# The row-maximum selector product of a fused attention and soft mixture-of-experts kernel, moved from fp32 to fp32r

## The chip, the cores and the metric

The kernel runs on one core of one Trainium2 chip. The metric is the device time of one execution in microseconds; the time before is 1116.34 us, the median of three runs (1116.29, 1116.34 and 1117.21).

## The reference, cut to what matters

There are B = 4 images with C = 128 channels. Keys and values are one and the same array: kv is averaged over 4 x 4 pixels, which leaves 768 keys for each image, and multiplied by a 128 x 128 matrix. Each of the 12288 queries of an image attends to its image's 768 keys. The result x (49152 rows of 128) goes through a soft mixture of experts with 8 experts of 4 slots.

```python
k = v = pool4x4(kv) @ w_sr
s = (q @ k.T) / sqrt(C)
s = s - s.max(-1)                      # the row maxima of this text
a = exp(s) / (exp(s).sum(-1) + 1e-9)
x = a @ v
logits = x @ phi                       # 32 slots
d = softmax(logits, over all rows)     # dispatch
c = softmax(logits, over the slots)    # combine
out = c @ experts(d.T @ x)             # two matrices and a ReLU each
```

## The kernel before, in words

The queries are worked through in 96 blocks of 512 (index i), 24 blocks to an image, and the blocks in groups of four (index g). Scores lie transposed: keys on the 128 partitions, queries along the free dimension, so a block has six score tiles of 128 x 512, in three PSUM buffers s0, s1, s2 of two tiles each. One block takes these steps.

- **Scores** (`qk`, L476 to L478): the query is split into a high fp32r part (`q_hi`, ACT, L462) and the remainder (`q_lo`, POOL, L466), likewise the key; three fp32r products make a tile, 18 a block.
- **Row maximum**: the maximum runs over keys, which lie on partitions. DVE reduces each pair of tiles with a reduction that transposes 32 x 32 squares (`rowmax1`, L483, three a block), then over the six tiles (`rowmax2`, L493). What is left is, in each of the four partition quadrants, the maximum over that quadrant's keys. To bring the four quadrants together, L495 spreads the result into a 128 x 64 tile `rq`, 16 columns for each quadrant and zero where the partition belongs to another quadrant, and one product on TensorE (`rowmax_pe`, L503) with the fixed 128 x 128 matrix `sel` (ones where two partitions have the same place in their quadrant) writes all four quadrants' values to every quadrant. Each output is a sum with one nonzero term. DVE takes the maximum of the four (`rowmax3`, L508) and transposes it out to 128 x 512 (`rowmax4`, L513).
- **Exponentials**: DVE subtracts the maximum from the scores (`sub`, L521, four instructions, after each of which a score buffer is nearer to being free for the next block), ACT makes the exponential twice, once as fp16 and once in fp32 (L528, L532), and POOL the fp16 remainder of it (`plo`, L537).
- **Values** (`av_hi`, `av_lo`, L554, L555, L562): about two blocks later, 72 fp16 products a block, evacuated by ACT (L572).

Once a group, a chain of small steps computes the dispatch weights (g0 to g7a, L596 to L713). Of these the text names the maximum over partitions (L631, L633), the small bf16 product with `sel_bf` (`g3m`, L654) that waits for `cb` from POOL (L647), the pass L718 for the combine weights, and the group's product L707. The groups' results go to experts and combine in a tail after the last block.

L503 is a float32 product. The program holds one instruction, the chip's profile shows two loads of weights and two matmuls for it.

The order on PE, DVE, ACT and POOL is fixed when the program is built: every step is entered with `op(engine, cost, latency, priority, dependencies, ...)`, and the class `Plan` plays the steps through on those costs and emits each engine's steps in the order in which they came out. Steps marked `hot` (L493 to L513) are preferred: the plan fits in other work before one only where it ends in time. At run time every engine works strictly in that order and waits with semaphores. The cost entered for L503 is 0.27 (L954).

Of the kernel before, what the change touches and what calls it, by code (L numbers as in the profile page):

```python
# [9 lines left out]
F32 = mybir.dt.float32  # L10
F32R = mybir.dt.float32r
# [9 lines left out]
P = 128  # L21
# [12 lines left out]
class Plan:  # L34
# [13 lines left out]
    def op(self, eng, cost, lat, prio, deps, fn, acq=(), use=(), at=0.0, slack=0.0, hot=False, raw=0.0):  # L48
        n = len(self.ops)
        if eng != "PE" and any(ring == "m" for ring, _ in use):  # L50
            prio -= URGE
        for key in list(acq) + list(use):
            self.users.setdefault(key, []).append(n)
        self.ops.append((eng, cost, lat, prio, list(deps), fn, list(acq), at, slack, hot, raw, list(use)))
        return n
# [117 lines left out]
def attention_then_soft_moe(ctx: ExitStack, tc: tile.TileContext, qT, kv0, kvT, w_sr, w_srT, phi, w1, w2, outT):  # L173
    nc = tc.nc
# [29 lines left out]
    cp = ctx.enter_context(tc.tile_pool(name="cp", bufs=1))  # L204
# [4 lines left out]
    sp = es.enter_context(tc.tile_pool(name="sp", bufs=2))  # L209
# [27 lines left out]
    NQD = P // Q32  # L237
    sel1 = cp.tile([P, Q32], F32, tag="sel1", name="sel1")
    nc.vector.tensor_reduce(out=sel1, in_=ident.rearrange("p (k j) -> p j k", k=NQD), axis=X, op=ALU.add)
    sel = cp.tile([P, P], F32, tag="sel", name="sel")  # L240
    nc.vector.tensor_copy(
        sel.rearrange("p (k j) -> p k j", k=NQD), sel1.unsqueeze(1).broadcast_to([P, NQD, Q32])
    )
    sel_bf = cp.tile([P, P], BF16, tag="sel_bf", name="sel_bf")
    nc.vector.tensor_copy(sel_bf, sel)
    quad = cp.tile([P, NQD], F32, tag="quad", name="quad")
# [16 lines left out]
    MX = {}  # L263
# [7 lines left out]
    NBK = BQ // Q32  # L271
# [6 lines left out]
    op = plan.op  # L278
# [41 lines left out]
    def kv_acc(b, c):  # L320
        if c == 0:
            kvs[b] = kvp.tile([P, KVC, NK], F32, tag="kv", name=f"kva_{b}")
            nc.sync.dma_start(out=kvs[b], in_=kvT[b - 1, :, :KVC, :])
        else:
            nc.gpsimd.dma_start(
                out=kvs[b], in_=kvT[b - 1, :, c * KVC : (c + 1) * KVC, :], accum_op=ALU.add,
                max_dma_last_dim=4 * 2 * NK,
            )
# [160 lines left out]
    def rowmax2(i):  # L489
        top = banks[plan.bank][:, 512 - (NQD + 1) * NBK :]  # L490
        pq = PQ[i] = top[:, NBK:]
        r1 = top[:, :NBK]
        nc.vector.tensor_reduce(out=r1, in_=MX[i].rearrange("p t b -> p b t"), axis=X, op=ALU.max)  # L493
        rq = sp.tile([P, NQD, NBK], F32, tag="rq", name=f"rq_{i}")
        nc.vector.tensor_tensor(  # L495
            out=rq, in0=r1.unsqueeze(1).broadcast_to([P, NQD, NBK]),
            in1=quad.unsqueeze(2).broadcast_to([P, NQD, NBK]), op=ALU.mult,
        )
        MX[i] = rq

    def rowmax_pe(i):
        pqv = PQ.pop(i)
        nc.tensor.matmul(pqv, sel, MX[i].rearrange("p k b -> p (k b)"), start=True, stop=True)  # L503
        MX[i] = pqv

    def rowmax3(i):
        m1 = sp.tile([P, NBK], F32, tag="m1", name=f"m1_{i}")
        nc.vector.tensor_reduce(out=m1, in_=MX[i].rearrange("p (k b) -> p b k", k=NQD), axis=X, op=ALU.max)  # L508
        MX[i] = m1
# [423 lines left out]
    for i in range(NB):  # L933
        b, ib = divmod(i, BPB)
        T0 = HEAD + i * PER
# [6 lines left out]
        for t in range(NT):  # L942
# [5 lines left out]
            if t % 2:  # L948
                ops["r", i, u] = op(
                    "DVE", dve(2 * BQ) + 0.02, 0.08, T0 - 2.0 + 0.65 * t, [ops["qk", i, t], ops["qk", i, t - 1]] + ([ops["r", i, u - 1]] if u else []),  # L950
                    lambda i=i, u=u: rowmax1(i, u), acq=[("r6", i)] if u == 0 else [], use=[(f"s{u}", i)] + ([("r6", i)] if u else []),
                )
        r2 = op("DVE", 0.36, 0.08, T0 + 2, [ops["r", i, NU - 1]], lambda i=i: rowmax2(i), acq=[("m", ("pq", i)), ("rq", i)], use=[("r6", i)], hot=True, raw=0.14)
        pe = op("PE", 0.27, 0.3, T0 - 10, [r2], lambda i=i: rowmax_pe(i), use=[("m", ("pq", i)), ("rq", i)], hot=True)  # L954
        r3 = op("DVE", 0.12, 0.08, T0 - 10, [pe], lambda i=i: rowmax3(i), acq=[("m1", i)], use=[("m", ("pq", i))], hot=True)
        r4 = op("DVE", dve(BQ) - 0.03, 0.08, T0 - 10, [r3], lambda i=i: rowmax4(i), acq=[("mb", i)], use=[("m1", i)], hot=True, raw=0.14)
        for t, n in ((0, 2), (2, 1), (3, 1), (4, 2)):
# [23 lines left out]
        for k in range(TB):  # L981
            m = px[k]
            p = T0 + AVD * PER + 1.3 * k
# [12 lines left out]
        if ib == 2 and b + 1 < B:  # L996
            nb = b + 1
            dep = [ops["av", i - 3]] if i >= 3 else []
            p = [op("SP", 0.1, 11.0, T0, [ops["s", i, 0]], lambda nb=nb: kv_acc(nb, 0), acq=[("kv", nb)])]
# [20 lines left out]
    for g in range(len(GB)):  # L1020
        n = nt(g) * NS
        p = HEAD + (GB[g][0] + GB[g][1] + KLAG) * PER
# [165 lines left out]
    for g in range(len(GB)):  # L1188
        n = nt(g) * NS
        p = T1 + 288 + 4 * g  # L1190
# [4 lines left out]
    for g, (o, n) in enumerate(chunks):  # L1195
        p = T1 + 300 + 4 * g
# [56 lines left out]
```

## Time and profile before

| | |
|---|---|
| median of three runs | 1116.34 us |
| profiled execution, first to last instruction (its span) | 1112.9 us |
| what lies around the span (median less span) | 3.4 us |
| stage of the 96 blocks | about 28 to 1010 us |
| PE busy between 300 and 900 us | 591.74 of 600 us |
| TensorE clock granted, mean over the span | 0.976 |

The profile gives no time of its own for the profiled execution beside its span; the runs' median is what stands nearest to it. PE is TensorE's matmuls, PEld its loads of weights, which overlap with matmuls; DVE is VectorE, ACT ScalarE, POOL GpSimd. In a timeline a row gives start and duration in us, and the start of the next row of the same engine tells when the engine was free to go on: a matmul's duration holds the way through the array as well, so 0.23 us stands at a product that is followed by the next one 0.07 us later. A number in brackets at a row's end is the time that the engine was idle before it, and what ended it.

### The profile page before, as it was taken

What the parts mean: (1) busy time and instruction counts of PE and PEld (TensorE: products, weight loads), DVE (VectorE), ACT (ScalarE), POOL (GpSimd) and SP (SyncE); (2) the same over time, 40 slices, a digit from 0 to 9 for tenths busy, and PEclk for the clock granted to TensorE, in tenths of its full rate; (3) what the DMA queues carried; (4) which work ended last, traced back from release to release, by engine and by line L of the source; (5) the groups of instructions that cost most, each with busy time, mean ns of one, the idle gap of its engine ahead of it and who ended that gap; (6) DMA issues with size and microseconds to landing.
All of it is one profiled execution on the core that took longest, in us unless ns stands there. A gap on an engine that the chain in (4) does not pass through costs nothing.

```text
span 1112.9 us, 24732 instructions
## 1 busy us (share of the span) xinstructions
PE 1044.9 (94%) x10198; PEld 893.6 (80%) x10198; DVE 984.2 (88%) x1493; ACT 829.4 (75%) x1029; POOL 870.5 (78%) x503
## 2 busy tenths in 40 slices
PE   3699999999999999999999999999999999997885
PEld 2588888888888888888888888888888888886343
DVE  7889889899889989899888988989989988997894
ACT  1677778778777878778777788688778777875563
POOL 0679898798899889789899989789889889873440
PEclk9899999999999999999999999999999999999975
DMA  9218301111136310120145310120110110113498
GB/s 351 108 31 177 70 16 39 39 58 39 39 60 150 82 35 6 39 87 10 39 102 108 82 39 1 39 95 2 39 39 1 39 39 2 39 39 114 145 406 357
DMA packets 17407, 89.15 MB, mean 80 GB/s; under 512 B 1680, under 2 KB 3984, under 8 KB 11152
## 3 DMA queue, kind: packets, MB, share of 16 engines
q1 hardware_dynamic: 13408, 69.47, 17.0%
q0 software_dynamic: 3312, 17.70, 8.4%
q8 instruction: 81, 1.33, 0.5%
q10 hardware_dynamic: 576, 0.41, 0.1%
q14 instruction: 30, 0.25, 0.1%
HBM read 58.87 MB, written 25.17 MB: 76 GB/s over the span
## 4 chain that ended last, share of the span: by engine, by line
PE 61%; ACT 18%; DVE 15%; issue 3%; POOL 2%; DMA 1%; SPq 0%; DVEq 0%; ACTq 0%
PE m L562 10%; PE m L554 10%; PE m L555 9%; ACT phi L528 8%; PE s L476 8%; PE s L478 7%; PE s L477 7%; ACT t L532 7%; DVE t L521 4%; PE m L503 3%; DVE r L483 3%; PE m L707 2%; PE po L1138 2%; DVE o L1147 2%; DVE mb L513 1%
## 5 line engine op out<-in xcount | busy, mean ns | idle before, releaser
L537 POOL TENSOR_TENSOR plo<-t,phi 128x1536 f16<-128x1536 f32 x190 | 598.8, 3156 | 128.1 <-ACT t L532 127.3
L528 ACT ACTIVATE phi<-t,lnk 128x1536 f16<-128x1536 f32 x192 | 301.5, 1570 | 118.9 <-DVE t L521 118.7
L483 DVE TRANSPOSE_TENSOR_REDUCE r<-s 128x32 f32<-128x1024 f32 x288 | 348.6, 1233 | 29.3 <-PE s L478 25.7
L554 PE MATMUL m<-vhi,phi 128*128 128x161 f16 x2280 | 354.7, 234 | 2.8 <-DVE acc L713 1.4
L555 PE MATMUL m<-vlo,phi 128*128 128x160 f16 x2280 | 353.8, 233 | 0.0
L521 DVE TENSOR_TENSOR t<-s,mb 128x1024 f32<-128x1024 f32 (+1 forms) x384 | 342.8, 949 | 9.3
L532 ACT ACTIVATE t<-t,lnk 128x1536 f32<-128x1536 f32 x192 | 301.5, 1570 | 3.6
L476 PE MATMUL s<-qhi,khi 128*128 128x512 f32 x576 | 239.9, 417 | 6.1 <-DVE t L521 5.8
L554 PEld LDWEIGHTS <-phi 128*128 128x128 f16 x2304 | 224.3, 98 | 24.3 <-issue 24.3
L555 PEld LDWEIGHTS <-phi 128*128 128x128 f16 x2304 | 225.1, 98 | 5.4 <-issue 3.5
L562 PE MATMUL m<-vhi,plo 128*128 128x161 f16 x2280 | 226.5, 234 | 0.4 <-POOL plo L537 0.4
L478 PE MATMUL s<-qhi,klo 128*128 128x512 f32 x576 | 226.6, 393 | 0.0
L477 PE MATMUL s<-qlo,khi 128*128 128x512 f32 x576 | 226.1, 392 | 0.0
L562 PEld LDWEIGHTS <-plo 128*128 128x128 f16 x2304 | 178.2, 100 | 1.2 <-POOL plo L537 0.6
L466 POOL TENSOR_TENSOR qlo<-q,qhi 128x512 fp32r<-128x512 f32 x96 | 128.6, 1340 | 26.8 <-ACT qhi L462 26.8
L572 ACT ACTIVATE xl<-m 128x322 f32<-128x322 f32 x189 | 81.4, 430 | 84.5 <-PE m L562 83.8
L476 PEld LDWEIGHTS s<-qhi,khi 128*128 128x128 f32 x576 | 109.2, 190 | 32.6 <-issue 7.5
L478 PEld LDWEIGHTS s<-qhi,klo 128*128 128x128 f32 x576 | 108.8, 189 | 24.7 <-DVE klo L356 0.5
L477 PEld LDWEIGHTS s<-qlo,khi 128*128 128x128 f32 x576 | 109.5, 190 | 18.7 <-issue 0.7
L513 DVE STREAM_TRANSPOSE mb<-m 128x512 f32<-128x512 f32 x96 | 68.3, 711 | 3.3
L462 ACT ACTIVATE qhi<-q 128x512 fp32r<-128x512 f32 x96 | 59.1, 616 | 1.5 <-issue 0.8
L508 DVE TENSOR_REDUCE m<-m 128x16 f32<-128x64 f32 x96 | 21.5, 224 | 40.7 <-PE m L503 40.7
(145 smaller groups left out, 860.1 us busy)
## 6 DMA issues: line engine op xcount, KB each, us to landing
q<-qT SPq DMA_DIRECT2D x23, 1024.0 KB, 4.8
outT<-o SPq DMA_DIRECT2D x21, 1024.0 KB, 5.4
kva<-kvT POOLq DMA_DIRECT2D x9, 1536.0 KB, 11.2
kva<-kvT SPq DMA_DIRECT2D x3, 1536.0 KB, 10.5
kv<-kv SPq DMA_DIRECT2D x8, 512.0 KB, 5.6
w<-w SPq DMA_DIRECT2D x2, 1536.0 KB, 6.4
w<-w SPq DMA_DIRECT2D x4, 768.0 KB, 4.4
outT<-o SPq DMA_DIRECT2D x6, 512.0 KB, 4.7
```

What stands on the lines that cost most here:

```text
L466: nc.gpsimd.tensor_tensor(out=lo, in0=q_src(i), in1=hi.bitcast(F32), op=ALU.subtract)
L476: nc.tensor.matmul(s, khi[:, ks], hi, start=True, stop=False)
L477: nc.tensor.matmul(s, khi[:, ks], lo, start=False, stop=False)
L478: nc.tensor.matmul(s, klo[:, ks], hi, start=False, stop=True)
L483: nc.vector.tensor_reduce(out=MX[i][:, 2 * u : 2 * u + 2, :].rearrange("p t b -> p (t b)"), in_=S[i, u].rearrange("p t (b j) -> p (t b) j" ...
L521: nc.vector.tensor_tensor(out=TT_[i, h][:, o : o + n, :], in0=S[i, t // 2][:, u : u + n, :], in1=MX[i].unsqueeze(1).broadcast_to([P, n, BQ ...
L528: nc.scalar.activation(hi, TT_[i, h], AF.Exp, bias=lnk, scale=SCALE)
L532: nc.scalar.activation(t, t, AF.Exp, bias=lnk, scale=SCALE)
L537: eng.tensor_tensor(out=lo, in0=TT_.pop((i, h)), in1=PP[i, h], op=ALU.subtract)
L554: nc.tensor.matmul(px, p, vhi[:, t, :], start=(t == 0), stop=False)
L555: nc.tensor.matmul(px[:, 1:], p, vlo[:, t, :], start=False, stop=False)
L562: nc.tensor.matmul(px, PP[i, t // TH][1][:, t % TH, ks], vhi[:, t, :], start=False, stop=(t == NT - 1))
```

## The change

A second copy of the selector matrix is made at the start in fp32r (`sel_r`, one copy on DVE), `rq` is written as fp32r by the same DVE instruction, and the product takes `sel_r` in place of `sel`. `sel` stays for the other users. The maximum is thereby rounded to fp32r; all scores of a row are reduced by the same rounded value. The cost that the plan assumes for the product falls from 0.27 to 0.16.

```diff
@@ setup
+    sel_r = cp.tile([P, P], F32R, tag="sel_r", name="sel_r")
+    nc.vector.tensor_copy(sel_r, sel)
     sel_bf = cp.tile([P, P], BF16, tag="sel_bf", name="sel_bf")
     nc.vector.tensor_copy(sel_bf, sel)
@@ rowmax2
-        rq = sp.tile([P, NQD, NBK], F32, tag="rq", name=f"rq_{i}")
+        rq = sp.tile([P, NQD, NBK], F32R, tag="rq", name=f"rq_{i}")
@@ rowmax_pe
-        nc.tensor.matmul(pqv, sel, MX[i].rearrange("p k b -> p (k b)"), start=True, stop=True)
+        nc.tensor.matmul(pqv, sel_r, MX[i].rearrange("p k b -> p (k b)"), start=True, stop=True)
@@ the plan's entry
-        pe = op("PE", 0.27, 0.3, T0 - 10, [r2], lambda i=i: rowmax_pe(i), ...)
+        pe = op("PE", 0.16, 0.3, T0 - 10, [r2], lambda i=i: rowmax_pe(i), ...)
```

Lines of the changed kernel from the new copy on stand two higher: L503 becomes L505. The 96 products keep their places; the plan's other cost moves some steps of the groups by one to a few places, about blocks 8 to 15, 32 to 36, 49 to 51, 56 to 60 and 73 to 75, and two exponentials at the end. The instructions of SyncE stay as they are.

On DVE in the setup, before, with the pooling of the first image's kv (L314) around the copies of the selector:

```order
L241 COPY sel<-sel_102 128x128
L314 TENSOR_TENSOR pool_129<-pool_129,kv_125 128x1024
L245 CAST sel_bf<-sel 128x128
L314 TENSOR_TENSOR pool_129<-pool_129,kv_125 128x1024 x2
L314 TENSOR_TENSOR pool_129<-pool_129,kv_137 128x1024 x2
```

and in the changed kernel:

```order
L241 COPY sel<-sel_102 128x128
L316 TENSOR_TENSOR pool_131<-pool_131,kv_127 128x1024
L245 CAST sel_r<-sel 128x128
L247 CAST sel_bf<-sel 128x128
L316 TENSOR_TENSOR pool_131<-pool_131,kv_127 128x1024 x2
```

The new copy stands directly ahead of the bf16 one, in the middle of the pooling.

On POOL in the first group, before (plo is the remainder of the exponential, qlo that of the query, cb the operand of the group's small product):

```order
L537 TENSOR_TENSOR plo_0_993<-t_0_930,phi_0_965 128x1536
L647 TENSOR_TENSOR cb_1020<-cq_991,cb_1020 128x4
L325 DMA kva_430<-kvT 128x2x1536
L537 TENSOR_TENSOR plo_1_1068<-t_1_959,phi_1_999 128x1536
L673 TENSOR_TENSOR D_1117<-LL,mrun_1095 128x512
L466 TENSOR_TENSOR qlo_1042<-q_306,qhi_1041 128x512
```

and in the changed kernel:

```order
L539 TENSOR_TENSOR plo_0_995<-t_0_933,phi_0_966 128x1536
L539 TENSOR_TENSOR plo_1_1042<-t_1_960,phi_1_993 128x1536
L649 TENSOR_TENSOR cb_1039<-cq_1014,cb_1039 128x4
L468 TENSOR_TENSOR qlo_1051<-q_308,qhi_1050 128x512
L327 DMA kva_432<-kvT 128x2x1536
L675 TENSOR_TENSOR D_1130<-LL,mrun_1122 128x512
```

cb comes one plo later, qlo ahead of the DMA and of D. On PE the small product that takes cb (L654, now L656) moves from the value products to the place behind the next block's first score tile.

On ACT at the start of the third image (about block 50), before (phi and t are the two exponentials, D and da the group's, qhi the query's high part):

```order
L532 ACTIVATE t_0_6829<-t_0_6829,lnk 128x1536
L682 ACTIVATE D_6882<-D_6882 128x512
L684 ACTIVATE da_6884<-da_6884 128x32
L528 ACTIVATE phi_1_6917<-t_1_6869,lnk 128x1536
L462 ACTIVATE qhi_6941<-q_5976 128x512
L532 ACTIVATE t_1_6869<-t_1_6869,lnk 128x1536
L572 ACTIVATE xl_6687<-m_114 128x322
```

and in the changed kernel:

```order
L534 ACTIVATE t_0_6831<-t_0_6831,lnk 128x1536
L530 ACTIVATE phi_1_6903<-t_1_6871,lnk 128x1536
L684 ACTIVATE D_6884<-D_6884 128x512
L686 ACTIVATE da_6886<-da_6886 128x32
L534 ACTIVATE t_1_6871<-t_1_6871,lnk 128x1536
L574 ACTIVATE xl_6689<-m_117 128x322
L464 ACTIVATE qhi_6970<-q_5978 128x512
```

D stands one phi later, and qhi one t and one evacuation (xl) later. The start of the fourth image (about block 74) reads the same way.

More of the change, by code (lines that the diff above doesn't have):

```diff
@@ L953, in attention_then_soft_moe @@
         r2 = op("DVE", 0.36, 0.08, T0 + 2, [ops["r", i, NU - 1]], lambda i=i: rowmax2(i), acq=[("m", ("pq", i)), ("rq", i)], use=[("r6", i)], hot=True, raw=0.14)
-        pe = op("PE", 0.27, 0.3, T0 - 10, [r2], lambda i=i: rowmax_pe(i), use=[("m", ("pq", i)), ("rq", i)], hot=True)
+        pe = op("PE", 0.16, 0.3, T0 - 10, [r2], lambda i=i: rowmax_pe(i), use=[("m", ("pq", i)), ("rq", i)], hot=True)
         r3 = op("DVE", 0.12, 0.08, T0 - 10, [pe], lambda i=i: rowmax3(i), acq=[("m1", i)], use=[("m", ("pq", i))], hot=True)
```

## The prediction

> **What bounds the kernel now.** First the page: the engines' shares and the chain that ended last. Then the stretches of the steady part, 300 to 900 us, and last the product's own line.
>
> ```profile
> PE 1044.9 (94%) x10198; PEld 893.6 (80%) x10198; DVE 984.2 (88%) x1493; ACT 829.4 (75%) x1029; POOL 870.5 (78%) x503
> PE 61%; ACT 18%; DVE 15%; issue 3%; POOL 2%; DMA 1%; SPq 0%; DVEq 0%; ACTq 0%
> ```
>
> ```profile
> 300.00:600.00 300.00, 295.46 (x2954) 259.81 (x2952) 272.07 (x404) 236.75 (x287) 263.32 (x150) 1.00 0.27 64
> 600.00:900.00 300.00, 296.27 (x2968) 260.01 (x2967) 270.39 (x399) 239.17 (x290) 260.89 (x149) 1.00 0.12 37
> ```
>
> In the steady part PE is busy 98 to 99% of the time at the full granted clock (1.00), DVE 90%, POOL 87%, ACT 79%. PE and DVE both matter: DVE's shortfall is partly a fixed wait, once a block, for the product in question.
>
> ```profile
> L503 PEld LDWEIGHTS m<-rq,sel x192: 186/188/190, 30.2 to 1003.9; 128*128 128x128 f32 x192
> L503 PE MATMUL m<-rq,sel x192: 275/284/323, 30.2 to 1004.0; 128*128 128x64 f32 x192
> ```
>
> ```profile
> DVE m L508 <- PE m L503: 40.7, 74, 0.6
> ```
>
> So 96 products are 192 loads and 192 matmuls, and in 74 of the 96 blocks DVE stood and waited for the result, 0.55 us on average. In the remaining 22 it had something else to do. These two numbers carry the forecast: the product lies on two paths, as time that PE spends and as time that DVE waits.
>
> **What one product costs now.** A block in which DVE waits, from the timeline:
>
> ```profile
> 625.25 0.22 DVE L495 TENSOR_TENSOR rq<-m,quad 128x64 f32<-128x64 f32 x1
> 625.59 0.30 PEld L503 LDWEIGHTS m<-rq,sel 128*128 128x128 f32 x2
> 625.62 0.41 PE L503 MATMUL m<-rq,sel 128*128 128x64 f32 x2
> 625.87 0.45 PE L562 MATMUL m<-vhi,plo 128*128 128x161 f16 x4
> 626.07 0.22 DVE L508 TENSOR_REDUCE m<-m 128x16 f32<-128x64 f32 x1 [0.59 <-PE m L503]
> ```
>
> The pair starts at 625.62 and PE goes on with L562 at 625.87: 0.25 us. The two loads span 0.30 and one lasts 0.19, so the second begins 0.11 after the first. The two matmuls span 0.41 and the second lasts 0.275 (the least of the row above), so it begins 0.135 after the first and holds PE for 0.25 - 0.135 = 0.115. L508 starts 0.04 after the pair's end (625.62 + 0.41 = 626.03).
>
> **What one fp32r product will cost.** No row shows one of 64 columns. The nearest are the score products, fp32r on both sides:
>
> ```profile
> 507.47 0.19 PEld L476 LDWEIGHTS s<-qhi,khi 128*128 128x128 f32 x1 [0.24 <-PE m L562]
> 507.50 0.47 PE L476 MATMUL s<-qhi,khi 128*128 128x512 f32 x1
> 507.81 0.39 PE L477 MATMUL s<-qlo,khi 128*128 128x512 f32 x1
> 508.04 0.39 PE L478 MATMUL s<-qhi,klo 128*128 128x512 f32 x1
> ```
>
> Each is one load and one matmul, so the pair does become one. L477 to L478 is 0.23 us for 512 columns, 0.45 ns a column. The first after fp16 work, as our product is, takes 0.31: 0.08 more, the part of its load (again 0.19 long) that nothing hides. A single product of 64 columns then holds PE for 0.08 + 64 x 0.45 ns = 0.11 us. That is one end: 0.25 - 0.11 = 0.14 saved. The other is that what remains is just like the first of the present pair, 0.135: 0.115 saved. I take 0.125, between ends that are close. DVE's wait shortens by the same amount, since the way from the last matmul's start to L508 is unchanged.
>
> The Trainium skill ("FP8 and Floating Point Precision", TensorE Precision Notes) says that a true FP32 product takes four passes through the array and that the reduced kind truncates its operands to 22 bits. An estimate from that page alone, three passes of 64 columns less at the 0.45 ns above, is 0.086 us a product, which would make 1110.2 of the sum below. The trace agrees on a pair that is dearer than one product, but shows it as two instructions with two loads, and I keep the rows' 0.125.
>
> **Where the saving reaches the end.** The blocks differ in a cycle of four, for the groups' work falls on some. In one kind DVE fills the wait:
>
> ```profile
> 594.51 0.22 DVE L495 TENSOR_TENSOR rq<-m,quad 128x64 f32<-128x64 f32 x1
> 594.66 0.68 DVE L718 TENSOR_REDUCE RM<-LL 128x16 f32<-128x512 f32 x1
> 594.89 0.41 PE L503 MATMUL m<-rq,sel 128*128 128x64 f32 x2 [0.44 <-ACT t L532]
> 595.33 0.23 DVE L508 TENSOR_REDUCE m<-m 128x16 f32<-128x64 f32 x1
> ```
>
> (The idle 0.44 is put down to ACT, but the product started just after rq ended at 594.73; rq it waited for.) PE stood before the product, so DVE sets the pace here, and DVE was in L718 until 594.66 + 0.68 = 595.34, when the pair's result was there anyway. A quicker product gives this block nothing: L718 is late next. PE gets its 0.125, and waits that much longer for the next rq. In the kind that follows two blocks later PE sets the pace:
>
> ```profile
> 611.29 1.25 DVE L483 TRANSPOSE_TENSOR_REDUCE r<-s 128x32 f32<-128x1024 f32 x1 [0.95 <-PE s L478]
> 615.67 0.23 DVE L495 TENSOR_TENSOR rq<-m,quad 128x64 f32<-128x64 f32 x1
> 615.96 0.43 PE L503 MATMUL m<-rq,sel 128*128 128x64 f32 x2
> 616.43 0.22 DVE L508 TENSOR_REDUCE m<-m 128x16 f32<-128x64 f32 x1 [0.53 <-PE m L503]
> ```
>
> DVE waits 0.95 for scores, and no idle time stands at L503: PE comes to it straight from the value products, and the time that PE saves on the product brings everything behind it forward. The other two kinds look like 625: rq ends, the product runs at once, DVE waits. There the path runs rq, product, and from it both PE and DVE go on sooner. So three blocks of four gain, on whichever path, and I count the 74 of the waits row: 74 x 0.125 = 9.25 us.
>
> **The new copy.** It stands in the setup's pooling, which DVE works off without a break and for which PE's first key product waits.
>
> ```profile
> 9.43 0.22 DVE L241 COPY sel<-sel 128x128 f32<-128x128 f32 x1
> 9.56 1.22 DVE L314 TENSOR_TENSOR pool<-pool,kv 128x1024 f32<-128x1024 f32 x1
> 10.49 1.41 POOL L466 TENSOR_TENSOR qlo<-q,qhi 128x512 fp32r<-128x512 f32 x1 [8.96 <-ACT qhi L462]
> 10.70 1.29 DVE L245 CAST sel_bf<-sel 128x128 bf16<-128x128 f32 x1
> 11.90 1.21 DVE L314 TENSOR_TENSOR pool<-pool,kv 128x1024 f32<-128x1024 f32 x1
> ```
>
> A copy of this size moves DVE on by 9.56 - 9.43 = 0.13 us, or by 11.90 - 10.70 = 1.2 where, as the times suggest, it is held until POOL's qlo ends at 11.90. The new copy would sit through that hold in sel_bf's place, and sel_bf behind it would be the quick one. I take 0.2 us, between 0.13 and 1.2. Writing rq as fp32r I put at nothing, by the two DVE rows of one operation and size, of which the first writes fp32r (683 ns) and the second fp32 (680):
>
> ```profile
> L1126 DVE TENSOR_TENSOR clo<-m,chi 128x512 fp32r<-128x512 f32 x23 | 15.6, 683 | 4.8 <-ACT chi L1122 4.8
> L521 DVE TENSOR_TENSOR t<-s,mb 128x512 f32<-128x512 f32 x192 | 122.9, 680 | 0.0
> ```
>
> **The moved steps.** In the first group cb, which POOL began at 101.48, comes one plo (3.1 us) later, about 104.6, and is done at 104.8. PE's small product L654 moves from 103.30 to behind the score tile that begins at 105.01, about 105.7, so PE should just not wait.
>
> ```profile
> 98.42 3.12 POOL L537 TENSOR_TENSOR plo<-t,phi 128x1536 f16<-128x1536 f32 x1
> 101.48 0.21 POOL L647 TENSOR_TENSOR cb<-cq,cb 128x4 bf16<-128x4 f32 x1
> 103.30 0.19 PE L654 MATMUL m<-cb,sel_bf 128*128 128x4 bf16 x2
> 105.01 0.48 PE L476 MATMUL s<-qhi,khi 128*128 128x512 f32 x1
> ```
>
> On ACT at the third and fourth image qhi comes behind one t and one evacuation.
>
> ```profile
> 523.14 0.61 ACT L462 ACTIVATE qhi<-q 128x512 fp32r<-128x512 f32 x1
> 523.66 1.56 ACT L532 ACTIVATE t<-t,lnk 128x1536 f32<-128x1536 f32 x1
> 525.13 0.41 ACT L572 ACTIVATE xl<-m 128x322 f32<-128x322 f32 x1
> 528.57 1.30 POOL L466 TENSOR_TENSOR qlo<-q,qhi 128x512 fp32r<-128x512 f32 x1
> ```
>
> The two take 2.0 us, and POOL did not read qhi until 528.57, 4.8 us after it was done, so the delay is hidden. Queued behind it on ACT are only the next exponentials. I put the moves at 0, with 1 us to either side for each place that is not quite covered (the first group and the two images), since an earlier step can as well gain: -3 to +3.
>
> **The sum.** 9.25 saved, less 0.2: 9.05 us. The profiled span of 1112.9 becomes 1103.85; the median of the runs stands 3.4 above the span and I leave that as it is: 1116.34 - 9.05 = 1107.3 us. The ends of the price give 74 x 0.14 = 10.4 and 74 x 0.115 = 8.5; with the copy's 0.13 and 1.2 and the moves that is 1103.1 to 1112.0.
>
> **The rivals.**
>
> - *PE alone sets the pace.* Then all 96 products count, 96 x 0.125 = 12.0 less 0.2: 1104.5. For it speaks PE's 98 to 99%, against it the idle 0.44 in front of the product at 594.89. 6%.
> - *Narrow fp32r is slow.* The score rows have 512 columns; at 64 an fp32r product may stream at a quarter of that rate, 64 x 1.8 ns = 0.115, and with 0.08 for the load hold PE for 0.195. Saved are 0.055 x 74 = 4.1, less 0.2: 1112.4. Nothing in the rows excludes it; that the fp32 pair needs no more than 0.115 for its second product, load included, makes it unlikely. 12%.
> - *The load gets quick.* If the load of a lone fp32r product were hidden wholly, as those of the fp16 products are, another 0.08 x 74 = 5.9 would go: 1101.4. The rows above speak against it, fp32r loads last 0.19 like fp32's. 2%. The Trainium skill ("TensorE: Matmul & The Clock Gate", Weight-path perf modes) has a rule of this kind: loads of 128 weights are fast where the type is not FP32. By that rule fp32r might count as fast; the trace's 0.19 disagrees.
> - *The moves eat it.* PE waits a whole plo (3.1) for cb in the first group, and at each of two images the 2.0 us of qhi are not covered: 7.1 lost of 9.05, 1114.4. Against it the 4.8 us of cover. 6%: within 0.2%.
> - *Slower: an fp32r product has a floor.* If the 0.31 of the first score product were a fixed price of going over to fp32r and back, and not a matter of columns, L505 would hold PE for 0.31 against 0.25, and DVE's wait would grow by as much: 0.06 x 74 = 4.4, plus 0.2: 1120.9. It decides from the point where one fp32r product takes over 0.25 us to the next. For it: no narrow fp32r row. Against: the next ones, without the change of type, take 0.23 for eight times the columns. 4%.
> - That it doesn't happen, the product still being split, is covered by the score rows: fp32r products have one record each.
>
> **How the numbers follow.** The likeliest case, 1107.3, has 70%. Faster are also PE alone, narrow fp32r and the quick load: 70 + 6 + 12 + 2 = 90%. Within 0.2% (2.2 us, about what a measurement of this kernel can tell from no change) are the moves, 6%; slower the floor, 4%. The range goes from 1103.1, the good end of the likeliest case, to 1112.8, which takes in narrow fp32r with 0.4 more for the copy.
>
> **What would show it.** In the changed profile L505 has 96 loads and 96 matmuls; from its start to the next L564 there are 0.11 to 0.135 us; DVE's wait for it falls from 0.53 and 0.59 to some 0.40 and 0.47 in the blocks of 625's kind; L510 starts at L720's end in the blocks of 594's kind, and PE's idle time there grows. Steady blocks of 625's kind begin sooner by 0.125 each. Wrong would be: over 0.19 us from L505 to L564, or an idle PE in front of L656 or of the first score product about blocks 9, 50 and 74.

## The result, and the profile after

The changed kernel takes 1103.7 us (median of four runs, 1102.28 to 1104.64) against 1116.32 for the kernel before on the same chip. The ratio is 0.9879, with a 95% interval of 0.9867 to 0.9891 (the plain quotient of these two medians is 0.9887). On two further chips the same kernel gave 0.9890 (0.9877 to 0.9904) and 0.9880 (0.9867 to 0.9892). The forecast was 1107.3 with a range from 1103.1 to 1112.8. The direction was right and the size too small: 12.6 to 13.4 us were gained where 9.05 were expected. The median lies 0.6 us inside the quick end of the range, and 0.9879 of 1116.34 is 1102.8, 0.3 us outside it.

The changed kernel's profiled execution took 1102.28 us, and its span is 1100.5. Time less span is 1.8 us in every run of every kernel here. The execution of before that was profiled, with its span of 1112.9, was therefore one of some 1114.7 us, as quick as the quickest of that kernel's later runs (1114.74 to 1118.7). The profiled execution of after is likewise the quickest of its four. So spans (12.4 less) and medians tell much the same.

The profile's page after begins so; the chain that ended last is its second line:

```profile
PE 1028.4 (93%) x10102; PEld 879.2 (80%) x10102; DVE 982.6 (89%) x1494; ACT 826.7 (75%) x1029; POOL 871.8 (79%) x503
PE 60%; ACT 18%; DVE 16%; POOL 3%; issue 2%; DMA 1%; SPq 0%; DVEq 0%; ACTq 0%
```

In the steady part PE is as full as before (the columns are the stretch and its length, then PE, PEld, DVE, ACT and POOL busy, then the granted clock, the DMA share and GB/s):

```profile
300.00:600.00 300.00, 295.40 (x2957) 258.84 (x2956) 273.98 (x409) 240.65 (x293) 267.30 (x153) 1.00 0.29 67
600.00:900.00 300.00, 296.32 (x2972) 259.48 (x2969) 273.46 (x402) 239.42 (x291) 260.29 (x147) 1.00 0.13 38
```

The product's own line has halved in number, and DVE's wait for it has fallen from 0.55 us on average (40.7 over 74) to 0.43 (30.3 over 71):

```profile
L505 PEld LDWEIGHTS m<-rq,sel_r x96: 186/186/187, 30.2 to 992.7; 128*128 128x128 f32 x96
L505 PE MATMUL m<-rq,sel_r x96: 267/269/299, 30.2 to 992.7; 128*128 128x64 f32 x96
```

```profile
DVE m L510 <- PE m L505: 30.3, 71, 0.5
```

A block in which DVE waits, from the timeline after (it answers to the one at 625 before), and behind the "..." a block in which DVE fills the wait (it answers to 594):

```profile
618.39 0.22 DVE L497 TENSOR_TENSOR rq<-m,quad 128x64 fp32r<-128x64 f32 x1
618.76 0.27 PE L505 MATMUL m<-rq,sel_r 128*128 128x64 f32 x1
618.87 0.61 PE L564 MATMUL m<-vhi,plo 128*128 128x161 f16 x6
619.07 0.23 DVE L510 TENSOR_REDUCE m<-m 128x16 f32<-128x64 f32 x1 [0.45 <-PE m L505]
...
588.40 0.23 DVE L497 TENSOR_TENSOR rq<-m,quad 128x64 fp32r<-128x64 f32 x1
588.54 0.68 DVE L720 TENSOR_REDUCE RM<-LL 128x16 f32<-128x512 f32 x1
588.77 0.27 PE L505 MATMUL m<-rq,sel_r 128*128 128x64 f32 x1 [0.46 <-ACT t L534]
589.13 0.22 DVE L510 TENSOR_REDUCE m<-m 128x16 f32<-128x64 f32 x1
```

From L505 to the next L564 there are 0.11 us where 0.25 stood. In the first block DVE waits 0.45 instead of 0.59. In the second, L510 follows the product's start after 0.36 us, where before it was 0.44 (595.33 - 594.89): this block has gained 0.08 too, although DVE's L720 fills the wait. L510 starts 0.59 after L720 started, earlier than L720's recorded end at 588.54 + 0.68 = 589.22. So here the end of a DVE row is not the moment from which DVE can go on.

**Where the time went, block by block.** The start of rq marks each block on DVE, 96 times:

```profile
L495 DVE TENSOR_TENSOR rq<-m,quad x96: 223/224/226, 29.9 to 1003.5; 128x64 f32<-128x64 f32 x96
```

```profile
L497 DVE TENSOR_TENSOR rq<-m,quad x96: 224/224/226, 29.9 to 992.5; 128x64 fp32r<-128x64 f32 x96
```

From the first to the last rq 11.1 us are gained; the last 1.3 of the 12.4 fall behind the last rq (109.3 us from there to the end before, 108.05 after). The step from one rq to the next, before less after, is the gain of a block. Its medians by kind of block in the cycle of four are 0.12, 0.135 and 0.13 us where DVE waits and 0.085 where the wait is filled, 0.47 for four blocks. Only two steps differ from their kind by over 0.2 us: one at block 27 (0.22 lost instead of 0.13 gained) and one at block 56 (0.5 gained).

### The profile page after: what moved, and what is told of

Same layout as the page of the kernel before. It is cut to its first block, busy times and chain, and to the rows that moved or that the text cites. A ratio compares the mean times of both kernels' runs of the same rounds, so it can differ in the third digit from the quotient of the medians.

```text
span 1100.5 us, 24542 instructions
## 1 busy us (share of the span) xinstructions
PE 1028.4 (93%) x10102; PEld 879.2 (80%) x10102; DVE 982.6 (89%) x1494; ACT 826.7 (75%) x1029; POOL 871.8 (79%) x503
## 4 chain that ended last, share of the span: by engine, by line
PE 60%; ACT 18%; DVE 16%; POOL 3%; issue 2%; DMA 1%; SPq 0%; DVEq 0%; ACTq 0%
PE m L564 11%; PE m L556 10%; PE m L557 10%; ACT phi L530 8%; PE s L478 8%; PE s L479 7%; PE s L480 7%; ACT t L534 7%; DVE t L523 4%; DVE r L485 3%; PE m L709 2%; DVE o L1149 2%; PE m L505 2%; POOL plo L539 1%; DVE mb L515 1%
## 5 line engine op out<-in xcount | busy, mean ns | idle before, releaser
L564 PE MATMUL m<-vhi,plo 128*128 128x161 f16 x2280 | 227.7, 234 | 0.4 <-POOL plo L539 0.4
L564 PEld LDWEIGHTS <-plo 128*128 128x128 f16 x2304 | 169.9, 98 | 1.2 <-POOL plo L539 0.6
L749 POOL TENSOR_TENSOR LL<-LL,RM 128x512 f32<-128x512 f32 (+2 forms) x25 | 24.8, 1013 | 32.6 <-DVE RM L744 32.6
## 6 DMA issues: line engine op xcount, KB each, us to landing
kva<-kvT POOLq DMA_DIRECT2D x9, 1536.0 KB, 10.8
```

The source lines that it names most:

```text
L564: nc.tensor.matmul(px, PP[i, t // TH][1][:, t % TH, ks], vhi[:, t, :], start=False, stop=(t == NT - 1))
```

## The experiments

The theories: A, the product alone makes the gain, in all blocks though less in the filled ones, and the moved steps are worth nothing; B, with the prediction's count, 74 blocks gain and the moves bring the rest; C, PE alone sets the pace, so every block gains alike. In the table "blocks" is what lies between the rq of block 2 and the rq of block 95, before less the kernel (52.55 to 1003.54 before, 52.23 to 992.45 after). This leaves out the head and the tail, which differ between executions of one kernel (below).

| kernel | ratio, 95% interval | median us | gain in the blocks, us |
|---|---|---|---|
| the change | 0.9879 (0.9867, 0.9891) | 1103.70 | 10.8 |
| the change again | 0.9890 (0.9877, 0.9904) | 1103.88 | 10.9 |
| the change, third time | 0.9880 (0.9867, 0.9892) | 1103.12 | 11.0 |
| fp32r, old order | 0.9911 (0.9897, 0.9924) | 1106.97 | 8.8 |
| the same again | 0.9904 (0.9891, 0.9916) | 1106.01 | 8.9 |
| fp32r, old order, kva's DMAs spaced out | 0.9890 (0.9877, 0.9904) | 1103.85 | 10.9 |
| fp32r, new cost, DMA earlier | 0.9939 (0.9923, 0.9954) | 1108.78 | 5.2 |
| fp32, new order | 1.0002 (0.9993, 1.0011) | 1117.13 | -0.6 |
| fp32, kva's DMAs spaced out | 0.9996 (0.9987, 1.0006) | 1115.66 | -0.1 |
| fp32r product twice | 0.9983 (0.9974, 0.9992) | 1114.58 | 1.6 |
| fp32 product twice | 1.0174 (1.0159, 1.0190) | 1136.24 | -20.6 |
| bf16 product | 0.9799 (0.9785, 0.9812) | 1094.04 | 20.1 |
| bf16 product, plan's cost 0.04 | 0.9795 (0.9782, 0.9808) | 1093.41 | 20.6 |

### The product without the moves, and the moves without the product

The changed kernel with the plan's old cost, so that every step keeps its old place:

```diff
-        pe = op("PE", 0.16, 0.3, T0 - 10, [r2], lambda i=i: rowmax_pe(i), ...)
+        pe = op("PE", 0.27, 0.3, T0 - 10, [r2], lambda i=i: rowmax_pe(i), ...)
```

> The fp32r product, with the plan's cost left at 0.27, so that every step stands where it stood before. Theory A (the product alone, gaining 0.136 us in the 73 blocks in which DVE waits and 0.08 in the 22 in which L718 or another step fills the wait): 9.9 + 1.8 = 11.7 us saved, ratio to before 0.9885 to 0.9905. Theory B (as predicted, the filled blocks gain nothing and the moved steps bring the rest): 74 x 0.125 = 9.25 saved, ratio 0.9915 to 0.9925. Theory C (PE alone sets the pace, all 96 products count in full): 96 x 0.136 = 13.1, ratio 0.988.

And the kernel before with the new cost alone, the order of the change with the fp32 product:

```diff
-        pe = op("PE", 0.27, 0.3, T0 - 10, [r2], lambda i=i: rowmax_pe(i), ...)
+        pe = op("PE", 0.16, 0.3, T0 - 10, [r2], lambda i=i: rowmax_pe(i), ...)
```

> The fp32 pair with the plan's cost at 0.16, so that only the moved steps are left of the change. Theory A and C: within 1 us of before, ratio 0.999 to 1.001. Theory B: 2 to 3.5 us faster, ratio 0.997 to 0.998.

Measured: 0.9911 and 1.0002. The two don't add up: the product alone brings about 10 us, the order alone nothing, both together 12.6 or more. 0.9911 lies between the ranges of A and B, so the steps from block to block have to decide. (The order alone gains 0.4 at block 56 and loses nearly as much at each of blocks 19 and 52.) The gain by kind of block in the first run is the change's own (0.08 where the wait is filled; 0.11, 0.13 and 0.13 where DVE waits), so the order does not touch the ordinary blocks. What the run lacks is mainly one step: from block 31 to block 32 it loses 1.3 us. The timeline of POOL and PE there (the second L656 takes the half of cb that POOL writes, the first the half that ACT writes):

```profile
344.48 1.20 POOL L327 DMA_DIRECT2D kva<-kvT  x1 [3.22 <-DMA kva<-kvT]
345.26 3.56 POOL L539 TENSOR_TENSOR plo<-t,phi 128x1536 f16<-128x1536 f32 x1
347.51 0.17 PE L656 MATMUL m<-cb,sel_bf 128*128 128x4 bf16 x1
348.33 0.64 POOL L649 TENSOR_TENSOR cb<-cq,cb 128x4 bf16<-128x4 f32 x1
349.03 0.16 PE L656 MATMUL m<-cb,sel_bf 128*128 128x4 bf16 x1 [1.35 <-POOL cb L649]
```

POOL issues the loads of the next image's kv itself (L327), in chunks into one buffer. It stands 3.22 us because the chunk before has not landed; behind it in POOL's queue wait plo and then cb; and PE waits 1.35 for cb with everything queued behind it. At block 56 it waits another 0.62, and the two together, 2.0 us, are what the run's blocks gain less than the change's (8.8 against 10.8). In the change at the same place cb stands ahead of the DMA:

```profile
344.88 0.21 POOL L649 TENSOR_TENSOR cb<-cq,cb 128x4 bf16<-128x4 f32 x1
345.02 1.18 POOL L327 DMA_DIRECT2D kva<-kvT  x1
345.79 3.56 POOL L539 TENSOR_TENSOR plo<-t,phi 128x1536 f16<-128x1536 f32 x1
346.60 0.19 PE L656 MATMUL m<-cb,sel_bf 128*128 128x4 bf16 x2
```

No one waits. That made a new theory, M: the moves are worth 2 to 3 us, but only because they keep a stall away that the quicker product would otherwise run into. Its rival R: the difference lies in chips and executions.

### Is it the wait for the DMA?

First the old order, with the loads held back by the plan (the delay before a chunk's pooling step grows):

```diff
-    ... lambda nb=nb, c=c: kv_acc(nb, c), use=[("kv", nb)], slack=10.0, raw=10.0))
+    ... lambda nb=nb, c=c: kv_acc(nb, c), use=[("kv", nb)], slack=10.0, raw=14.0))
```

> The fp32r product with the plan's old cost of 0.27, as in the run with the old order, but the plan holds back the pooling step of kv that issues POOL's DMA (a raw delay of 14 in place of 10), which puts cb ahead of that DMA at blocks 32 and 56 as the new order does; a few other steps of POOL and DVE move with it. Theory M: the 3 us between the change and its form with the old order come from cb standing in POOL's queue behind a DMA that waits for its buffer, 1 to 2 us at each of blocks 32 and 56; then this kernel stands with the change, ratio 0.987 to 0.989, L656 has no idle PE ahead of it at the two blocks. Rival R: the 3 us come from elsewhere (other moved steps, the chips, or executions that differ), and this kernel stands with the old order, ratio 0.991, although the wait for cb is gone.

with the change itself on the same chip,

> The change itself once more, on the same chip as the other runs of this call. All theories: 0.986 to 0.990. Below 0.989 the moved steps keep a worth of 2 to 3 us over the old order (0.9911); at 0.990 to 0.991 that worth was the difference of chips and executions, and the product alone makes the gain (96 blocks by about 0.117 us = 11.2 us, ratio 0.990).

and the kernel before with the same edit:

> The kernel before, with its fp32 product, and the pooling step of kv held back as in the run with the old order and the late DMA. Theory M: if the wait for cb behind the DMA costs 1 to 2 us at blocks 32 and 56, the kernel before gains by the same move: 1.5 to 3 us, ratio 0.997 to 0.9985. Rival R: with the fp32 product the plan's old order waits 0.4 us at block 56 only, or PE's wait is made up for later, ratio 1.000 +- 0.001, as the run with the new order and the fp32 product gave 1.0002.

Measured: 0.9890, 0.9890 and 0.9996. The old order without the wait stands with the change: 10.9 us gained in the blocks by both. The change's 0.9890 lies between the two cases of its own expectation; the three runs on one chip further down decide between them. One point of the expectation was off: the DMA at block 32 still stands one plo ahead of cb, but 21 us behind the chunk before it (issued at 321.19, landed at 331.91), and the buffer is free when POOL comes to it:

```profile
342.25 1.20 POOL L327 DMA_DIRECT2D kva<-kvT  x1
343.37 3.24 POOL L539 TENSOR_TENSOR plo<-t,phi 128x1536 f16<-128x1536 f32 x1
346.44 0.32 POOL L649 TENSOR_TENSOR cb<-cq,cb 128x4 bf16<-128x4 f32 x1
348.15 0.19 PE L656 MATMUL m<-cb,sel_bf 128*128 128x4 bf16 x2
```

So it is the wait that counts and not the place. The fp32 kernel gains nothing by the same edit that its times could show, against M's 1.5 to 3 us: the kernel before hardly had the stall. Its list of waits has one entry for cb, at block 56, where its trace with the edit is 0.4 us quicker; the timeline shows POOL's wait for the chunk ahead of it:

```profile
PE m L654 <- POOL cb L647: 0.4, 1, 0.4
```

```profile
592.91 1.19 POOL L325 DMA_DIRECT2D kva<-kvT  x1 [2.24 <-DMA kva<-kvT]
597.46 0.16 PE L654 MATMUL m<-cb,sel_bf 128*128 128x4 bf16 x1 [0.41 <-POOL cb L647]
```

Then the other way about: the change's own cost, the chunks 1 us earlier in the plan, which puts the DMA ahead of cb again, in the first group too. Beside it the old order and the change once more, all three on one chip.

```diff
-    ... lambda nb=nb, c=c: kv_acc(nb, c), use=[("kv", nb)], slack=10.0, raw=10.0))
+    ... lambda nb=nb, c=c: kv_acc(nb, c), use=[("kv", nb)], slack=10.0, raw=9.0))
```

> The changed kernel with the plan's new cost, but the pooling step of kv held back less (a raw delay of 9 in place of 10), so that POOL's DMA of kva stands ahead of cb again at blocks 32 and 56, and in the first group too, while the other moved steps differ little. Theory M: the stall comes back, 1.4 us at block 32 and 0.6 at block 56, PE idle ahead of L656 there; 2 us over the change, ratio 0.9905 to 0.9915. Rival R: the difference between the change and its form with the old order lay in chips and executions (clock in the head and the tail), and this kernel stands with the change to 0.5 us whatever stands ahead of cb.

> The fp32r product with the plan's old cost, once more, on one chip with the change. Theory M: 2 us over the change, 1.4 of it lost at block 32 and 0.6 at block 56. Rival R: equal to the change within 0.5 us, and a step at block 32 is not seen again.

> The change once more, as the measure for the two above on the same chip: 0.988 to 0.990 by either theory; in the 96 blocks 11.2 us from the product (0.117 a block) and 0.4 to 0.5 at block 56 from cb.

Measured: 0.9939, 0.9904 and 0.9880. On one chip the old order is 2.9 us behind the change, and the early DMA 5.7. Their waits of PE for cb, of the early DMA first and of the old order behind it:

```profile
PE m L656 <- POOL cb L649: 4.0, 3, 1.7
```

```profile
PE m L656 <- POOL cb L649: 2.0, 2, 1.2
```

The change has no such row. The old order gains 2.1 us less in the blocks than the change, and its PE waits 2.0 for cb: theory M's 2 us, though as 0.8 and 1.2 at blocks 32 and 56 instead of 1.4 and 0.6. The early DMA gains 5.8 less and waits 4.0: 1.7 at block 8, 1.0 at 32 and 1.3 at 56. The rest was lost at block 56, and not in a wait: as PE went on there, the granted clock was halved for 3.4 us.

```profile
594.18 0.16 PE L656 MATMUL m<-cb,sel_bf 128*128 128x4 bf16 x1 [1.32 <-POOL cb L649]
```

```profile
594.20:597.60 3.40, 3.40 (x26) 3.40 (x26) 2.91 (x6) 0.00 (x0) 3.40 (x2) 0.50 1.05 214
```

An estimate from that row, half of 3.4, is 1.7 us, which with the 4.0 makes 5.7. In none of the other thirteen traces was the clock low between the rq of block 2 and that of block 95. That the wait brought the low clock on is likely by the place, but one execution doesn't show it. M holds and R falls; M's sizes for the early DMA were too small, for it counted neither block 8 nor the clock.

Why the stall is longer with the quicker product is settled only in part. The chunk for which POOL waits took longer: at blocks 32 and 56 it landed 11.0 and 11.6 us after its issue in the trace of before, and 12.0 to 12.9 in the two of the old order with fp32r. What makes the transfers longer was not tried.

### What the product costs

The changed kernel with its product issued twice into the same output:

```diff
         nc.tensor.matmul(pqv, sel_r, MX[i].rearrange("p k b -> p (k b)"), start=True, stop=True)
+        nc.tensor.matmul(pqv, sel_r, MX[i].rearrange("p k b -> p (k b)"), start=True, stop=True)
```

> The changed kernel with its fp32r product issued twice into the same output; the result is unchanged. Theory A: a product costs PE one exposed load plus its columns, 0.107 us in the changed kernel's rows, and a second one of the same weights costs the same, since the load is issued again: 96 x 0.107 = 10.3 us less what the filled blocks hide, 8 to 10.5 us over the changed kernel, ratio to the kernel before about 0.996 to 0.998. The pair of fp32 products should then differ from this pair by 0.243 - 0.214 = 0.03 us a block only, so the gain of the change is one load and one matmul taken out, and not the number format. Rival, the format: a first fp32r product behind fp16 work pays 0.08 us for the change of type and the second one does not, 64 columns at 0.45 ns = 0.03 us: 96 x 0.03 = 2.8 us over the changed kernel, ratio 0.990. Rival of the prediction's slower case: a floor of 0.3 us a product would give 96 x 0.3 = 29 us, ratio 1.013.

And the kernel before with its fp32 product issued twice, by the same edit:

> The kernel before with the fp32 product issued twice (the second writes the same result), so that 0.243 us more lie on both paths in every block. Theory A and C: in the filled blocks the pair's end and L718's end coincide before, so there it counts too: 96 x 0.243 = 23.3 us slower, 1139.6 us. The prediction's count of three blocks in four: 74 x 0.243 = 18.0, 1134.3 us.

Measured: 0.9983 and 1.0174. The first lies just above theory A's 0.996 to 0.998 and far from the rivals' 0.990 and 1.013. A second fp32r product of the same weights costs what the first does:

```profile
624.12 0.23 DVE L497 TENSOR_TENSOR rq<-m,quad 128x64 fp32r<-128x64 f32 x1
624.49 0.27 PE L505 MATMUL m<-rq,sel_r 128*128 128x64 f32 x1
624.59 0.28 PE L506 MATMUL m<-rq,sel_r 128*128 128x64 f32 x1
624.71 0.41 PEld L565 LDWEIGHTS <-plo 128*128 128x128 f16 x6
624.91 0.23 DVE L511 TENSOR_REDUCE m<-m 128x16 f32<-128x64 f32 x1 [0.57 <-PE m L506]
```

0.10 us to the second, 0.12 to what follows. The format rival (0.03 for the second) falls. Two fp32r products take 0.22 where the one fp32 product took 0.24 to 0.25, and nearly the whole gain is given back (1.6 of 10.8 us in the blocks are left): what the change saves is a load with its matmul, and the step from fp32 to fp32r as a number format next to nothing. With the fp32 product issued twice PE is held for 0.47 instead of 0.24, and every kind of block is longer by 0.22 to 0.23, the filled one too. That is the count of theories A and C with a smaller size: 20.6 us are lost in the blocks and 19.2 by the medians, against their 23.3 and the 18.0 of the prediction's count, by which the filled blocks would have lost nothing. A longer product is hidden in no kind of block; by a shorter one the filled blocks gain only 0.085.

### A still shorter product

The product in bf16 (rq and the selector; the maximum is rounded to bf16):

```diff
-        rq = sp.tile([P, NQD, NBK], F32R, tag="rq", name=f"rq_{i}")
+        rq = sp.tile([P, NQD, NBK], BF16, tag="rq", name=f"rq_{i}")
-        nc.tensor.matmul(pqv, sel_r, MX[i].rearrange("p k b -> p (k b)"), start=True, stop=True)
+        nc.tensor.matmul(pqv, sel_bf, MX[i].rearrange("p k b -> p (k b)"), start=True, stop=True)
```

> As the change, but rq is written as bf16 and the product takes the bf16 selector that the kernel has already; the maximum is rounded to bf16. Its weights are loaded by an instruction of their own, which need not wait for rq. Theory A: the product holds PE for 0.03 us as the group's bf16 product L654 does, DVE's wait of 0.39 to 0.45 falls by 0.08 to 0.16, the 22 filled blocks gain nothing (L720 is already what L510 waits for): 73 x 0.08 to 0.16 = 6 to 12 us under the change, 1092 to 1098 us. Theory C: all 96 gain at least the 0.08 of PE's time, 7.7 us, also where L720 fills the wait.

and the same with a cost of 0.04 in the plan:

> The product in bf16 (rq and the selector rounded to bf16) as in the bf16 run, and the plan told a cost of 0.04 for it. If the order still counts, the plan can use the shorter product and the time falls by 0 to 2 us below the bf16 run's ratio of 0.9799; if the plan's order is only moved by chance, the time moves by +-1 us and the ratio stays at 0.979 to 0.981.

Measured: 0.9799 and 0.9795; the plan's cost makes no difference here that the intervals could show. Both are quicker than the kernel before and than the change; the first by 9.7 us than the change, inside theory A's 6 to 12. A waiting block and, behind the "...", a filled one:

```profile
613.88 0.23 DVE L497 TENSOR_TENSOR rq<-m,quad 128x64 bf16<-128x64 f32 x1
614.16 0.20 PE L505 MATMUL m<-rq,sel_bf 128*128 128x64 bf16 x1
614.20 0.60 PE L564 MATMUL m<-vhi,plo 128*128 128x161 f16 x6
614.40 0.22 DVE L510 TENSOR_REDUCE m<-m 128x16 f32<-128x64 f32 x1 [0.30 <-PE m L505]
...
623.88 0.68 DVE L720 TENSOR_REDUCE RM<-LL 128x16 f32<-128x512 f32 x1
624.02 0.20 PE L505 MATMUL m<-rq,sel_bf 128*128 128x64 bf16 x1 [0.36 <-ACT t L534]
624.47 0.22 DVE L510 TENSOR_REDUCE m<-m 128x16 f32<-128x64 f32 x1
```

The product holds PE for 0.04 us and DVE waits 0.30. The three waiting kinds gain 0.30, 0.23 and 0.28 a block, the filled kind the same 0.085 as with fp32r: L510 again starts 0.59 after L720 did. This excludes C: from fp32r to bf16 PE saves as much in a filled block as in the others (0.07 us), and the block is no shorter for it. There, L720 is late next, after 0.085 us.

## Why the prediction came out short, point by point

- **One load and one matmul: right.** L505 has 96 of each.
- **The price: right.** The product holds PE for 0.108 us where 0.242 stood, and for 0.137 where 0.271 stood (where PE comes straight from the value products): 0.134 saved, inside the 0.115 to 0.14; the waiting blocks gain 0.12 to 0.135 each, 0.127 on average, where 0.125 was taken. The narrow product isn't slow, its load isn't hidden wholly (it still lasts 186 ns, and the product holds PE for 0.11 where the 64 columns alone would be 0.03 by the prediction's 0.45 ns), and there is no floor of 0.3, as the doubled product shows. The estimate worked out from the Trainium skill ("FP8 and Floating Point Precision", TensorE Precision Notes), 0.086 us a product, was further off: it left out the load that goes.
- **Which blocks gain: wrong, and this is the step that failed.** "A quicker product gives this block nothing: L718 is late next." The filled blocks gained 0.085 each, 23 x 0.085 = 2.0 us up to the last rq. The step took L718's recorded end (594.66 + 0.68 = 595.34), which met L508's start (595.33) to 0.01, for the time from which DVE was free. It was free 0.59 after L718's start, at 595.25; L508 was waiting for the product, and could gain 0.08 before L718 became the later of the two. Two readings of the prediction's own rows said so already. L508 starts 0.03 after the pair's end (594.89 + 0.41 = 595.30), as it starts 0.04 after it in the block at 625, where it waits. And of the rows quoted for the copy, L241 lasts 0.22, yet the next instruction starts 0.13 after L241's start. The Trainium skill ("VectorE: DVE Perf Modes", The DRAIN you can't avoid) says that the next instruction starts earlier than the pipeline has emptied where it is not held; by that the end of a row is no bound either, and the trace's 0.59 against 0.68 agrees.
- **The copy: 0.13 us on average, where 0.2 was taken.** In the trace of after it cost next to nothing: sel_r and sel_bf move DVE on by 0.13 each, the four pooling steps behind them take 5.94 instead of 4.99, and the pooling's result (`pooled`) is begun at 16.94 against 16.93 before. In six of the ten executions with the copy the hold falls on sel_r, as the prediction expected (1.28 us). From the start of the pooling step ahead of the copies to the start of `pooled` there are 7.27 to 7.37 us in the four fp32 executions, 7.38 in the four with the copy where the hold falls elsewhere, and 7.49 to 7.51 in these six.
- **The moved steps: right in sum, in part by luck.** Against the trace of before they bring 0.4 us at block 56 and lose 0.35 at block 27. The prediction looked at the first group and at qhi, and left out the third consequence of the new order: cb stands ahead of POOL's DMA at blocks 32 and 56. With the quick product and the old order, 2 to 3 us of the gain are lost there, as the experiments show: a stall that the prediction did not foresee was kept away by a move that it did not look at. A part of this was to be read before: PE's wait of 0.4 for cb at block 56, behind POOL's wait of 2.2 for a chunk.
- **The offset of 3.4 us: wrong, but without effect.** It is 1.8; the rest is how much quicker the profiled execution was than the median. The difference of medians (12.6) and the difference of spans (12.4) agree, so that the term cancels.

From the first to the last rq the sum then reads 72 x 0.127 = 9.1 (the three waiting kinds), 2.0 (the filled kind) and 0.1 (the moves): 11.2 us, against 11.1 measured and the prediction's 9.25, for the copy lies ahead of the first rq. In the blocks, then, the failed step is the whole shortfall.

It is not the whole shortfall of the medians. They say 12.6 to 13.4, with an interval of 1.3 to either side, 1.5 to 2.3 above the 11.1, and that remainder isn't assigned. In the spans, 1.3 of the 12.4 stand in the tail; of the two other traces of the change one has a tail of 108.4 us and one of 109.6, against 109.3 before, so that this part is the execution's and not the change's. The three other fp32 kernels too come out 0.5, 0.9 and 1.4 us better by the medians than in the blocks; a part of the remainder may be that the trace of before, from which the blocks are counted, is one of a quick execution. Whether an ordinary execution of the kernel before loses more at blocks 32 and 56 than the profiled one stays open; the fp32 kernel with the DMAs spaced out allows at most 1.5 us for that (0.9987).

## What to carry to other kernels

Where an engine's instruction ends just as another engine's result arrives, don't decide by the recorded ends which of the two is late. Look for a like instruction whose successor waits for nothing else, see how soon after its start the successor starts, and count from the start.

A stage made quicker can run into a transfer that does not get quicker with it, and a step of an in-order queue that waits for the transfer holds up everything behind. So look through the waits of all queues for ones that are a few tenths of a microsecond long or hidden today. A planner's cost that is brought into line with the new instruction may be worth a fifth of the gain through such a place, or nothing, as its further cut with bf16.

## What the runs showed of the hardware beside that

The head and the tail of one kernel differ by over a microsecond between executions, and the clock granted there differs with them. At 38 to 42 us the same program, the change, ran once at the full granted clock and once at 0.77; of the first execution and then of the second (the change again):

```profile
38.00:42.00 4.00, 2.04 (x10) 1.33 (x8) 3.60 (x5) 4.00 (x4) 3.03 (x1) 1.00 0.00 0
```

```profile
38.00:42.00 4.00, 3.21 (x11) 2.22 (x9) 2.89 (x3) 3.39 (x4) 2.70 (x1) 0.77 0.00 0
```

The second reached block 2 1.7 us later than the first, and the gain from there on was the same (10.8 and 10.9). The Trainium skill ("TensorE: Matmul & The Clock Gate", What's actually happening) says that the clock is decided in windows of about 3.4 us that run freely beside the kernel; the granted clock's low stretches behind the last rq, most of them 3.4, 6.8 or 13.7 us long, agree. Two traces are best compared between marks in the steady part.

In two of the three waiting kinds of block the bf16 product starts 0.06 us after rq's end (613.88 + 0.22 to 614.16) and the fp32r product 0.15 us (618.39 + 0.22 to 618.76). The row of the fp32r load itself starts only 0.12 after rq's end, and the matmul's 0.03 behind it:

```profile
618.73 0.19 PEld L505 LDWEIGHTS m<-rq,sel_r 128*128 128x128 f32 x1
```

In the third kind, where PE comes straight from the value products, both start 0.05 to 0.06 after rq's end, and the fp32r product holds PE 0.03 longer instead. What holds the load back in the first two isn't shown.
